# Row maxima turned in aligned groups and split off VectorE, sequence products kept for the last T blocks, and the output projection's operands loaded elsewhere

## The chip, the cores and the metric

The kernel runs on 1 core of one Trainium2 chip. The metric is the device time of one launch in microseconds; three runs of the kernel before gave 730.19, 731.53 and 732.51 us, a median of 731.53. The engines are named as in the profile: PE (matrix products; PEld its weight loads), DVE (VectorE), ACT (ScalarE), POOL (GpSimd) and SP (SyncE, which here only issues DMAs).

## The reference

Two mixers of one input x (2048 rows of 512) are added with a gate per row.

```python
def _A_ref(x, dft_seq_re, dft_seq_im, dft_hid_re, dft_hid_im):
    a = jnp.einsum("bsd,ed->bse", x, dft_hid_re)
    b = jnp.einsum("bsd,ed->bse", x, dft_hid_im)
    return jnp.einsum("ts,bse->bte", dft_seq_re, a) - jnp.einsum("ts,bse->bte", dft_seq_im, b)

def _B_ref(x, wqkv, wo):
    H = 32; Dh = D // H; W = 256
    ...
    scores = jnp.einsum("bhqd,bhkd->bhqk", q, k) * (Dh ** -0.5)
    mask = (idx[:, None] - idx[None, :] >= 0) & (idx[:, None] - idx[None, :] < W)
    p = _softmax(jnp.where(mask[None, None], scores, -1e9), axis=-1)
    o = jnp.einsum("bhqk,bhkd->bhqd", p, v)
    return (lambda x, *d: x.transpose(*d))(o, 0, 2, 1, 3).reshape(B, S, D) @ wo

g = _sigmoid((x * gate_w).sum(-1, keepdims=True))
return g * a + (1 - g) * b
```

A is a Fourier transform along the hidden and then the sequence dimension. B is attention with 32 heads of 16 in a window of 256 keys, and an output projection by wo.

## The kernel before

All large products take operands that are split into a high and a low part ("hl": a copy rounded to fp32r, and the rest), and add three of the four partial products (TERMS).

**Order.** One Python loop, `for n in range(N + LAG + 1)` (L938), writes the program out. N is 128: 8 sets of four heads by 16 blocks of 128 queries. Step n emits the four heads of **S block** n (`s_head`, L404: scores of one query block against its keys, and on DVE the row's extremum over the masked scores) and of **T block** n - 9 (`t_head`, L462: the scores again, transposed, with the row's extremum folded into the product by two more rows of the operand, and the exponential on ACT). LAG = 9 blocks lie between. From n = 128 there are T blocks alone. After four T blocks `pv` (L486) multiplies exponentials and values, once POOL has masked them (`t_mask`, L475).

Between the heads `fill` (L918) takes steps of a generator, `dense` (L672): first the q, k and v projections and the hidden transform, then ("proj" done) the sequence transform, 16 blocks of 24 steps (`c_block`, L646). One step is a pair of matmuls on the two halves of the rows (L246). The rate is a constant per stage (FILL_PROJ 1.55, FILL_SEQ 2.3 steps per half head). `defer(ticks, fn)` puts an instruction off by so many ticks, where each dense step is one tick and each half head 0.7: ticks set the place in the program, not a time. All engines work their own queue in order, and SP issues nearly all DMAs in order.

**Maxima.** `s_head` writes the four heads' extrema as columns of a 128x16 tile `nm`. Every four blocks `m_rows` (L424) negates them into a high part (L427, TENSOR_SCALAR) and a low part (L428, SCALAR_TENSOR_TENSOR), turns the 128x32 tile by a DVE transposition (L430), writes it to DRAM (m_scr) and 12 ticks later reads it back as rows 48 and 49 of `ring0`, where the T blocks' products take it. The groups begin at n = 9, 13, 17 and so on; one that crosses a sequence end is read in two parts.

**Projection.** The sum over the T blocks passes through DRAM: u_scr, packing into l_scr (row sums) and o_scr, reciprocals (L527), and back. For each quarter of the rows (sb 0 to 3) `o_load` (L841) loads four tiles of o and of the reciprocals, multiplies them on DVE 16 ticks later (L854) and splits them on ACT (L102) and DVE (L105); sb 1 and 2 start when the sequence products are done ("seq"), sb 3 when attention is. `wo_run` (L873) then makes output block tb: 12 matmuls, and one DVE instruction that adds the gated transform r (L893), which `wo_get` loads from r_scr into `fin` (in ring0's place) by SP.

Of the kernel before, what the change touches and what calls it, by code (L numbers as in the profile page):

```python
# [21 lines left out]
NS = 8  # L22
# [6 lines left out]
NPT = 7  # L29
FILL_FIRST, FILL_PROJ, FILL_SEQ = 4.0, 1.55, 2.3  # L30
TERMS = ((0, 0), (0, 1), (1, 0))
# [20 lines left out]
def fnet_window_mix(ctx: ExitStack, tc: tile.TileContext, xT, x, wqk, wv, wm, wx, cc, wo, gw, out):  # L52
# [14 lines left out]
    c_scr = [[dram.tile([P, U_W], F32, name=f"c_scr{c}_{q}") for q in range(4)] for c in range(4)]  # L67
    m_scr = [dram.tile([2, 2, 2, 4, 4, 32], F32, name=f"m_scr{i}") for i in range(NS * NB // 4 + 4)]
    l_scr = [[dram.tile([2, 16, 512], F32, name=f"l_scr{i}_{h}") for h in range(2)] for i in range(4)]
# [118 lines left out]
    for h in range(2):  # L188
        nc.gpsimd.memset(f(ring[1][64 * h + 32:64 * h + 64]), 1.0)

# [58 lines left out]
    def es_tile():  # L249
        return ev.tile([P, U_W], F32, name="es", bufs=3)  # L250

# [149 lines left out]

    ML = {}

    def s_head(n, j):  # L404
        p, h = divmod(j, 2)
        jb = n % NB
        u, jj = divmod(n - LAG, 4)
        if u not in ML:
            ML[u] = at.tile([P, 16], F32, name="nm")
            if not (0 <= LAG + 4 * u and LAG + 4 * u + 4 <= NS * NB):  # L410
                nc.vector.memset(ML[u], 0.0)
# [5 lines left out]
        nc.tensor.matmul(ps[:, :w], ring[0][r, p, jb * P:(jb + 1) * P], ring[1][r, p, k0:k0 + w],  # L417
                         start=True, stop=True)
        sm = at.tile([P, WIN], BF16, name="sm", bufs=1)
        nc.vector.tensor_tensor_reduce(out=sm[:, :w], in0=ps[:, :w], in1=mask[:, WIN - w:],  # L420
                                       scale=1.0, scalar=3e38, op0=OP.add, op1=OP.min,
                                       accum_out=ML[u][:, c:c + 1])

    def m_rows(u):  # L424
        m = ML.pop(u)
        hl = at.tile([P, 2, 16], F32R, name="mhl", bufs=1)
        nc.vector.tensor_scalar(hl[:, 0], m, -1.0, None, op0=OP.mult)  # L427
        nc.vector.scalar_tensor_tensor(hl[:, 1], m, -1.0, f(hl[:, 0]), op0=OP.mult, op1=OP.subtract)  # L428
        mt = at.tile([P, 32], F32, name="mt", bufs=1)
        nc.vector.transpose(mt, f(hl[:]).rearrange("q l c -> q (l c)"))  # L430
        ms = m_scr[u + LAG // 4 + 1]

        def write():
            ld(ms.rearrange("l h p b i q -> i (l h p b) q"), mt)
            defer(12, read)

        def read():
            b, end = max(0, LAG + 4 * u), min(NS * NB, LAG + 4 * u + 4)
            while b < end:
                e = min(end, (b // NB + 1) * NB)  # L440
                o = b - LAG - 4 * u
                for h in range(2):
                    ld(f(ring[0][64 * h + 48:64 * h + 50, :, b % NB * P:b % NB * P + (e - b) * P]),
                       ms[:, h, :, o:o + e - b].rearrange("l p b i q -> l p (b i q)"))
                b = e
        defer(2, write)

# [181 lines left out]

    order = CLEAR + [tb for p in PAIRED for tb in p]  # L630
    MRAW = {}
    MHL = {}
# [13 lines left out]
    def c_block(n, done):  # L646
        tb = order[n]
        clear = tb % 2 == 0
        pss = acc()
        hl = MHL.pop(n)  # L650
        m = 0
        for i in range(2):
            u = slice(0, H + 1) if i == 0 else slice(H, D + 1) if clear else slice(H + 1, 2 * H + 2)
            o = slice(H - 1, D) if clear and i else slice(0, H + 1)
            for q in range(4):
                k = (2 * q + i) * P
                for x, y in TERMS:
                    mm([ps[:, o] for ps in pss], hl[x][:, k:k + P], U[tb % 4, q][:, y, u], m == 0, m == 23,
                       True)
                    m += 1  # L660
# [180 lines left out]
    def o_load(sb, g):  # L841
        ls = l_scr[sb][g // 2]
        if sb == 3:
            t = pt_tile([P, 3, 512], F32R)
            o = f(t[:, 2])
        else:
            t = big_tile()[:, :, 0:512]
            o = f(t[:, 1])
        rl = RL[0][:, sb * 2 - 4 + g // 2, g % 2] if FIN and sb > 1 else es_tile()[:, 0:512]
        ld(rl, bass.AP(tensor=ls.tensor, offset=ls[1, g % 2 * 8].offset, ap=[[512, 8], [0, 16], [1, 512]]))  # L850
        ld(o, o_scr[sb][g])

        def product():
            nc.vector.tensor_mul(rl, o, rl)  # L854
            defer(4, high)

        def high():
            for c, p in TURNS:
                hi_of(by_class(t[:, 0])[:, c], rows_of(rl)[:, c, p])
            defer(4, low)  # L860

        def low():
            for c, p in TURNS:
                lo_of(by_class(t[:, 1])[:, c], rows_of(rl)[:, c, p], by_class(t[:, 0])[:, c])
            defer(8, OHL[sb].append, t)
        defer(16, product)

    def wo_get(tb):
        if tb in stored and tb not in wo_r:
            wo_r[tb] = FIN[0][:, tb % 8]  # L870
            ld(wo_r[tb], r_scr[tb])

    def wo_run():  # L873
# [11 lines left out]
        for q in range(0, 512, w):  # L885
# [7 lines left out]
            nc.vector.scalar_tensor_tensor(r[:, k], ps[:, :w], g0[:, tb:tb + 1], r[:, k], op0=OP.mult, op1=OP.add)  # L893
            defer(3 if tb == 15 else 8, ld, out[sb][:, c, k], r[:, k])
        wo_get(tb + 3)
# [211 lines left out]
```

## Time and profile before

| | us |
|---|---|
| median of 3 runs | 731.53 |
| profiled execution, its own time | 732.08 |
| its span in the trace | 730.2 |
| PE busy | 603.6 (83%) |
| DVE busy | 495.2 (68%) |
| POOL busy | 435.1 (60%) |
| ACT busy | 428.4 (59%) |

In the profile's rows "L427 DVE" is line 427 on VectorE; "out<-in" are the program's tile names; a bracket gives the idle time ahead of an instruction on its engine and what ended it. A matmul's end is modelled, so busy PE is not PE at its peak. In the windows, PEclk is the share of the TensorE clock that was granted. S blocks end at 619.8 us, the last T block's products at 662.0 us.

### The profile page before, as it was taken

How to read it: one execution, taken by the hardware profiler on the slowest of the kernel's cores; microseconds unless marked ns; L12 is line 12 of the kernel's file. 1: busy time of each engine (PE TensorE's matmuls, PEld its weight loads, DVE VectorE, ACT ScalarE, POOL GpSimd, SP SyncE). 2: the span in 40 equal slices, each digit the busy share in tenths (PEclk: the TensorE clock that was granted, in tenths of full speed). 3: DMA queues.
4: the chain of work that ended last, by engine and by line, in shares of the span. 5: the costliest groups of instructions: out<-in, count | busy, mean ns of one | idle time of the engine just before them, and what ended most of it. 6: DMA issues, size and time to landing. Idle time of an engine off the chain costs nothing. (4 is left out here: it accounts for less than half of the span.)

```text
span 730.2 us, 17617 instructions
## 1 busy us (share of the span) xinstructions
PE 603.6 (83%) x6222; PEld 450.6 (62%) x6222; DVE 495.2 (68%) x1419; ACT 428.4 (59%) x952; POOL 435.1 (60%) x521
## 2 busy tenths in 40 slices
PE   9999699899788898988868887769777799559885
PEld 6788466666454666665546566657666587437664
DVE  5278677787787788787766765675688677344561
ACT  6434578677556676665556767476667668652220
POOL 6012557676687766678584979988988746420000
PEclk9999889999999999889988897667779969858898
DMA  7777677787565778567586699856566743655883
GB/s 278 259 233 199 205 228 225 228 263 210 176 201 172 213 227 273 179 202 207 169 262 214 210 268 278 269 148 188 171 195 197 207 138 117 190 174 145 259 276 110
DMA packets 93605, 152.61 MB, mean 209 GB/s; under 512 B 33028, under 2 KB 42116, under 8 KB 93380
## 3 DMA queue, kind: packets, MB, share of 16 engines
q1 hardware_dynamic: 92068, 149.28, 66.9%
q10 hardware_dynamic: 1440, 2.10, 0.9%
q8 instruction: 53, 0.87, 0.6%
q14 instruction: 44, 0.36, 0.2%
HBM read 108.56 MB, written 47.24 MB: 213 GB/s over the span
## 5 line engine op out<-in xcount | busy, mean ns | idle before, releaser
L420 DVE CUSTOM_DVE_ANT_0 sm<-s,mask 128x384 bf16<-128x384 f32 (+2 forms) x512 | 270.3, 528 | 104.3 <-PE s L417 54.7
L473 ACT ACTIVATE pt<-t 128x384 f32<-128x384 f32 (+2 forms) x512 | 231.4, 474 | 101.1 <-PE t L472 77.8
L472 PE MATMUL t<-ring,ring 50*128 50x384 f32 (+2 forms) x512 | 218.3, 442 | 59.0 <-ACT pt L473 30.1
L246 PE MATMUL d<-big,hl 64*128 64x512 f32 (+2 forms) x1440 | 248.8, 384 | 0.5 <-DVE es L257 0.5
L417 PE MATMUL s<-ring,ring 48*128 48x384 f32 (+2 forms) x512 | 199.0, 400 | 33.0 <-DVE nm L420 28.7
L246 PEld LDWEIGHTS d<-big,hl 64*128 64x128 f32 x1440 | 177.0, 223 | 6.5 <-issue 1.7
L417 PEld LDWEIGHTS s<-ring,ring 48*128 48x128 f32 x512 | 106.2, 212 | 99.6 <-DVE nm L420 86.7
L479 POOL TENSOR_SCALAR_AFFINE_SELECT pt<-pt 128x512 f32<-128x512 f32 x128 | 83.0, 649 | 140.5 <-ACT pt L473 140.0
L472 PEld LDWEIGHTS t<-ring,ring 50*128 50x128 f32 x512 | 108.1, 214 | 91.3 <-ACT pt L473 46.4
L246 PE MATMUL d<-hl,big 64*128 64x512 f32 x600 | 111.7, 416 | 0.0
L498 PE MATMUL o<-pt,vpad 64*32 64x320 f32 (+5 forms) x2816 | 89.2, 392 | 15.9 <-POOL pt L479 10.8
L498 PEld LDWEIGHTS o<-pt,vpad 64*32 64x32 f32 x2816 | 69.1, 117 | 38.4 <-POOL pt L479 13.6
L339 POOL TENSOR_TENSOR cv<-cv 128x256 f32<-128x256 f32 (+1 forms) x64 | 74.4, 1163 | 20.4 <-DMA cv<-cc 16.9
L483 POOL TENSOR_SCALAR_AFFINE_SELECT pt<-pt 128x512 f32<-128x512 f32 x112 | 74.8, 667 | 0.0
L246 PEld LDWEIGHTS d<-hl,big 64*128 64x128 f32 x600 | 67.1, 195 | 4.8 <-issue 1.0
L504 ACT COPY es<-o 128x512 f32<-128x512 f32 x32 | 18.8, 586 | 82.0 <-PE o L498 77.9
L342 POOL TENSOR_TENSOR cv<-cv 128x512 f32<-128x512 f32 x48 | 62.9, 1311 | 0.0
L540 ACT ACTIVATE cv<-cv 128x768 f32<-128x768 f32 x72 | 60.6, 842 | 0.6 <-POOL cv L339 0.6
L505 DVE TENSOR_TENSOR es<-o,es 128x512 f32<-128x512 f32 x32 | 22.0, 688 | 43.2 <-ACT es L504 35.9
L105 POOL TENSOR_TENSOR hl<-es,hl 128x512 fp32r<-128x512 f32 x14 | 18.5, 1319 | 48.0 <-ACT hl L102 48.0
L105 POOL TENSOR_TENSOR hl<-raw,hl 128x512 fp32r<-128x512 f32 x35 | 45.4, 1309 | 2.2 <-ACT hl L102 2.2
L242 PE MATMUL t<-big 128*128 128x512 f32 x144 | 40.0, 438 | 8.1 <-DVE fin L893 8.1
(98 smaller groups left out, 648.3 us busy)
## 6 DMA issues: line engine op xcount, KB each, us to landing
cv<-cc SPq DMA_DIRECT2D x64, 512.0 KB
qk_scr<-hl SPq DMA_DIRECT2D x32, 512.0 KB
ring<-qk_scr SPq DMA_DIRECT2D x128, 128.0 KB
ring<-qk_scr SPq DMA_DIRECT2D x128, 64.0 KB
u_scr<-es SPq DMA_DIRECT2D x32, 256.0 KB
raw<-cc SPq DMA_DIRECT2D x16, 512.0 KB
fin<-r_scr SPq DMA_DIRECT2D x17, 256.0 KB
big<-c_scr SPq DMA_DIRECT2D x16, 258.0 KB
```

Of the source, the lines that this page charges most:

```text
L105: (nc.gpsimd if pool else nc.vector).tensor_sub(lo, raw, f(hi))
L246: nc.tensor.matmul(pss[h], w[r], x[r], start=start, stop=stop, skip_group_check=skip)
L339: (nc.gpsimd if pool else nc.vector).tensor_sub(out, a, b)
L342: (nc.gpsimd if pool else nc.vector).tensor_add(out, a, b)
L417: nc.tensor.matmul(ps[:, :w], ring[0][r, p, jb * P:(jb + 1) * P], ring[1][r, p, k0:k0 + w], start=True, stop=True)
L420: nc.vector.tensor_tensor_reduce(out=sm[:, :w], in0=ps[:, :w], in1=mask[:, WIN - w:], scale=1.0, scalar=3e38, op0=OP.add, op1=OP.min, accu ...
L472: nc.tensor.matmul(ps[:, :w], ring[1][r, p, q0:q0 + P], ring[0][r, p, q0:q0 + w], start=True, stop=True)
L473: nc.scalar.activation(pt[:, j, :w], ps[:, :w], AF.Exp, scale=-1.0)
L479: nc.gpsimd.affine_select(a, a, pattern=[[0, 4], [1, P]], compare_op=OP.is_ge, fill=0.0, base=0, channel_multiplier=-1)
L483: nc.gpsimd.affine_select(a, a, pattern=[[0, 4], [-1, P]], compare_op=OP.is_gt, fill=0.0, base=0, channel_multiplier=1)
L498: nc.tensor.matmul(ot[h][32 * j:32 * j + 32, a - sb * 512:e - sb * 512], v2[r, j], pt[r, j, a - kb * P:e - kb * P], start=kb == kbs[0], st ...
L540: nc.scalar.activation(junk, src, AF.Abs, accum_out=dst)
```

## The change

1. **Maxima.** The groups are aligned (n = 0, 4, 8 ...), and a group is turned at the start of the next block. DVE only transposes the raw 128x32 tile (one fixed tile NM, half of it zeros). ACT then copies the turned tile into the high part, POOL subtracts for the low part, and SP writes both, one DMA each; the reads are two per group. The constant rows of ring1 are -1 instead of 1, so nothing has to be negated.
2. **Sequence products.** In the S blocks the rate is set so that 48 steps are left at n = 128; these are spread over the last nine T blocks. After the last S block there are 49 steps in the program, where there were 36.
3. **Projection.** r for tb 0 to 2 is loaded from n = 132 on into the tiles T; for the other tb the load is issued by ACT. Of quarters 0 to 2 the reciprocals land in the high half of the operand tile and the product goes to an `es` tile, 24 ticks after the load. Stores of the output stand 13 ticks behind, not 8. A load of r_scr0 that was issued twice is issued once.

```diff
-FILL_FIRST, FILL_PROJ, FILL_SEQ = 4.0, 1.55, 2.3
+FILL_FIRST, FILL_PROJ, SEQ_END = 4.0, 1.55, 48
...
-        nc.gpsimd.memset(f(ring[1][64 * h + 32:64 * h + 64]), 1.0)
+        nc.gpsimd.memset(f(ring[1][64 * h + 32:64 * h + 64]), -1.0)
...
     def m_rows(u):
-        m = ML.pop(u)
-        hl = at.tile([P, 2, 16], F32R, name="mhl", bufs=1)
-        nc.vector.tensor_scalar(hl[:, 0], m, -1.0, None, op0=OP.mult)
-        nc.vector.scalar_tensor_tensor(hl[:, 1], m, -1.0, f(hl[:, 0]), op0=OP.mult, op1=OP.subtract)
         mt = at.tile([P, 32], F32, name="mt", bufs=1)
-        nc.vector.transpose(mt, f(hl[:]).rearrange("q l c -> q (l c)"))
+        nc.vector.transpose(mt, NM)
+        hl = at.tile([P, 2, 32], F32R, name="mhl", bufs=1)
+        defer(2, hi_of, hl[:, 0], mt)
+        defer(4, minus, hl[:, 1], mt, f(hl[:, 0]))
...
         def write():
-            ld(ms.rearrange("l h p b i q -> i (l h p b) q"), mt)
-            defer(12, read)
+            for l in range(2):
+                ld(ms[l].rearrange("z h p b i q -> i (z h p b) q"), f(hl[:, l]))
+            defer(9, read)
...
-        defer(2, write)
+        defer(7, write)
...
         for tb in range(3):
-            defer(1 + 6 * tb, wo_get, tb)
+            wo_get(tb)
...
-        rl = RL[0][:, sb * 2 - 4 + g // 2, g % 2] if FIN and sb > 1 else es_tile()[:, 0:512]
+        rl = RL[0][:, g // 2, g % 2] if sb == 3 else f(t[:, 0])
...
         def product():
-            nc.vector.tensor_mul(rl, o, rl)
-            defer(4, high)
+            to = rl if sb == 3 else es_tile()[:, 0:512]
+            nc.vector.tensor_mul(to, o, rl)
+            defer(4, high, to)
...
-        defer(16, product)
+        defer(16 if sb == 3 else 24, product)
...
-            wo_r[tb] = FIN[0][:, tb % 8]
-            ld(wo_r[tb], r_scr[tb])
+            wo_r[tb] = T[tb][:, 0:D] if tb < 3 else FIN[0][:, tb % 8]
+            (ld if tb < 3 else nc.scalar.dma_start)(wo_r[tb], r_scr[tb])
...
-            defer(3 if tb == 15 else 8, ld, out[sb][:, c, k], r[:, k])
+            defer(3 if tb == 15 else 13, ld, out[sb][:, c, k], r[:, k])
...
-        rate = FILL_FIRST if n < LAG else FILL_SEQ if "proj" in have else FILL_PROJ
+        if n < LAG:
+            rate = FILL_FIRST
+        elif "proj" not in have:
+            rate = FILL_PROJ
+        elif n < N:
+            rate = max(0, left[0] - SEQ_END) / (4 * (N - n) - 2)
+        else:
+            rate = left[0] / (4 * (N + LAG - n) - 2) if n < N + LAG else 0
...
+        if n >= N + 4:
+            for tb in range(3):
+                wo_get(tb)
...
+        if n % 4 == 0 and 0 < n <= N:
+            m_rows(n // 4 - 1)
...
-                defer(3, t_mask, k)
+                defer(3 if n < N else 1, t_mask, k)
...
-            if p == 0 and k % 4 == 0 and k // 4 - 1 in ML:
-                defer(3, m_rows, k // 4 - 1)
```

What this moves, as the built programs have it. First DVE at the end of a group of four blocks in the sequence stage (sm is the masked score, thrown away; nm the extrema), before:

```order
L420 ISA nm 128x1
L420 ISA sm,nm<-s,mask 128x256
L420 ISA nm 128x1
L427 TENSOR_SCALAR mhl<-nm 128x16
L428 SCALAR_TENSOR_TENSOR mhl<-nm,mhl 128x16
L430 STREAM_TRANSPOSE mt<-mhl 128x32
L420 ISA sm,nm<-s,mask 128x256
L420 ISA nm 128x1
```

and now, on DVE and then on POOL (pt are exponentials that are masked, cv blocks of the transform's matrices that are compared):

```order
L417 ISA sm,nm<-s,mask 128x384
L417 ISA nm 128x1
L423 STREAM_TRANSPOSE mt<-nm 128x32
L417 ISA sm,nm<-s,mask 128x384
L417 ISA nm 128x1
```

```order
L471 AFFINE_SELECT pt<-pt 128x4x128
L475 AFFINE_SELECT pt<-pt 128x4x128
L342 TENSOR_TENSOR cv<-cv 128x2x256
L339 TENSOR_TENSOR mhl<-mt,mhl 128x32
L339 TENSOR_TENSOR cv<-cv 128x2x128
L342 TENSOR_TENSOR cv<-cv 128x2x256
```

Two DVE instructions have gone, and the low part stands in POOL's queue among masks and comparisons. Second, ACT among the last T blocks (with buffer numbers; es_9787 and its like are products of the projection's operands, t the scores, o the attention's result), before:

```order
L473 ACTIVATE pt_9861<-t_9884 128x384
L102 CAST big_9786<-es_9787 128x384
L102 CAST big_9786<-es_9787 128x128
L473 ACTIVATE pt_9906<-t_9907 128x384
L473 ACTIVATE pt_9906<-t_9910 128x384
L102 CAST big_9845<-es_9846 128x384
L102 CAST big_9845<-es_9846 128x128
L473 ACTIVATE pt_9906<-t_9929 128x384
L473 ACTIVATE pt_9906<-t_9932 128x384
L749 ACTIVATE es_9939<-d0_9756 128x258
```

and now:

```order
L465 ACTIVATE pt_9869<-t_9893 128x384
L465 ACTIVATE pt_9869<-t_9896 128x384
L102 CAST big_9782<-es_9878 128x384
L102 CAST big_9782<-es_9878 128x128
L496 COPY es_9953<-o_9903 128x512
L465 ACTIVATE pt_9969<-t_9970 128x384
L465 ACTIVATE pt_9969<-t_9973 128x384
L102 CAST big_9812<-es_9958 128x384
L102 CAST big_9812<-es_9958 128x128
```

The first copies (CAST) of the projection's operands stand some three T blocks later; before, there are eight tiles of them ahead of the last T block's result, now four. Third, SP at the end of attention (u_scr3 is the last result's store), before:

```order
L96 DMA u_scr3_1_181<-es_10188 128x512
L96 DMA es_10193<-l_scr2_0_170 128x1x512
L96 DMA big_10192<-o_scr2_184 128x512
L96 DMA fin_10196<-r_scr0_186 128x512 x2
L96 DMA rl_10197<-l_scr2_1_171 128x1x512
L96 DMA big_10208<-o_scr2_184 128x512
L96 DMA fin_10196<-r_scr1_187 128x512
L96 DMA l_scr3_1_173<-u_scr3_1_181 16x512
```

and now:

```order
L96 DMA u_scr3_1_177<-es_10111 128x512
L96 DMA l_scr3_1_169<-u_scr3_1_177 16x512
L96 DMA o_scr3_181<-u_scr3_1_177 16x8192
L96 DMA l_scr2_1_167<-lt_10113 128x64
L96 DMA big_10148<-l_scr1_0_164 128x1x512
L96 DMA big_10148<-o_scr1_179 128x512
L96 DMA big_10151<-l_scr2_0_166 128x1x512
L96 DMA big_10151<-o_scr2_180 128x512
L96 DMA r_scr13_195<-ev_9884 128x512
```

The last quarter's packing has moved up, and the loads of quarters 1 (l_scr1, o_scr1) and 2, which stood among the T blocks, now come behind it. Fourth, DVE in the projection (es_10253 to es_10274 are products of quarters 1 and 2, rl those of quarter 3), now:

```order
L849 TENSOR_TENSOR es_10272<-big_10213 128x512
L849 TENSOR_TENSOR es_10274<-big_10216 128x512
L105 TENSOR_TENSOR pt_10225<-rl_10118,pt_10225 128x384
L105 TENSOR_TENSOR pt_10225<-rl_10118,pt_10225 128x128
L849 TENSOR_TENSOR rl_10118<-pt_10242,rl_10118 128x512
L105 TENSOR_TENSOR big_10213<-es_10272,big_10213 128x384
L105 TENSOR_TENSOR big_10213<-es_10272,big_10213 128x128
```

The product of quarter 3's second tile (pt_10242) stands ahead of the low part of quarter 1's last tile (big_10213); before, quarter 1 was through on DVE before the last T block's result.

More of the change, by code (lines that the diff above doesn't have):

```diff
@@ L67, in fnet_window_mix @@
     c_scr = [[dram.tile([P, U_W], F32, name=f"c_scr{c}_{q}") for q in range(4)] for c in range(4)]
-    m_scr = [dram.tile([2, 2, 2, 4, 4, 32], F32, name=f"m_scr{i}") for i in range(NS * NB // 4 + 4)]
+    m_scr = [dram.tile([2, 2, 2, 2, 4, 4, 32], F32, name=f"m_scr{i}") for i in range(NS * NB // 4)]
     l_scr = [[dram.tile([2, 16, 512], F32, name=f"l_scr{i}_{h}") for h in range(2)] for i in range(4)]
@@ L249, in es_tile @@
     def es_tile():
-        return ev.tile([P, U_W], F32, name="es", bufs=3)
+        return ev.tile([P, D], F32, name="es", bufs=3)
     def collect(pss, then, scale=1.0):
@@ L400, in u_split @@
         defer(4, lo_of, t[:, 1], f(t[:, 1]), t[:, 0], True)
-    ML = {}
+    NM = const.tile([P, 32], F32, name="nm")
+    nc.gpsimd.memset(NM, 0.0)
     def s_head(n, j):
@@ L406, in s_head @@
         jb = n % NB
[L407 to L411, printed above, removed]
+        u, jj = divmod(n, 4)
         c = (h * 2 + p) * 4 + jj
@@ L421, in s_head @@
                                        scale=1.0, scalar=3e38, op0=OP.add, op1=OP.min,
[L422 removed]
+                                       accum_out=NM[:, c:c + 1])
     def m_rows(u):
[L425 to L428 removed]
         mt = at.tile([P, 32], F32, name="mt", bufs=1)
[L430 to L431 removed]
+        nc.vector.transpose(mt, NM)
+        hl = at.tile([P, 2, 32], F32R, name="mhl", bufs=1)
+        defer(2, hi_of, hl[:, 0], mt)
+        defer(4, minus, hl[:, 1], mt, f(hl[:, 0]))
+        ms = m_scr[u]
         def write():
[L434 to L435 removed]
+            for l in range(2):
+                ld(ms[l].rearrange("z h p b i q -> i (z h p b) q"), f(hl[:, l]))
+            defer(9, read)
         def read():
[L438 to L445, printed above, removed]
[L446 removed]
+            b = u % 4 * 512
+            for h in range(2):
+                ld(f(ring[0][64 * h + 48:64 * h + 50, :, b:b + 512]), ms[:, 0, h].rearrange("l p b i q -> l p (b i q)"))
+        defer(7, write)
     PT = {}
@@ L630, in fnet_window_mix @@
     order = CLEAR + [tb for p in PAIRED for tb in p]
+    left = [16 * 24]
     MRAW = {}
@@ L659, in c_block @@
                        True)
+                    left[0] -= 1
                     m += 1
```

10 lines of the change are left out of this document (5 added, 5 removed).

## The prediction

> **What bounds the kernel now.** I read the windows first, then the PE's waits stage by stage, then the timelines at the longest waits. In the windows each engine has its busy time and count; PEclk is the granted clock.
>
> ```profile
> core 0: us, PE busy (x) PEld busy (x) DVE busy (x) ACT busy (x) POOL busy (x), PEclk, DMA share, GB/s
> 456.00:476.00 20.00, 13.74 (x175) 11.97 (x175) 14.29 (x24) 10.64 (x24) 20.00 (x24) 0.67 0.83 250
> 596.00:616.00 20.00, 18.60 (x260) 14.23 (x241) 13.62 (x47) 13.67 (x31) 9.43 (x14) 0.95 0.42 130
> 619.80:640.00 20.20, 11.45 (x190) 9.31 (x187) 8.66 (x18) 13.95 (x34) 8.39 (x13) 0.80 0.62 185
> 640.00:662.00 22.00, 14.86 (x207) 10.87 (x207) 9.64 (x16) 11.21 (x28) 5.16 (x8) 0.50 0.51 161
> 662.00:706.00 44.00, 35.89 (x134) 27.11 (x134) 22.98 (x39) 11.45 (x19) 0.00 (x0) 0.91 0.73 231
> 706.00:730.20 24.20, 15.48 (x72) 12.77 (x70) 5.55 (x9) 0.00 (x0) 0.00 (x0) 0.80 0.46 156
> ```
>
> There are three stages. Up to 619.8 us S blocks (with their maxima) and T blocks (exponentials) run together, and the PE is the fullest engine wherever nothing stalls (18.60 of 20 us). From 619.8 to 662.0 only T blocks are left and the PE is half idle. From 662.0 the output projection runs, up to 730.2. These are the PE's waits in the first stage (total us, times, longest):
>
> ```profile
> PE s L417 <- DVE nm L420: 28.7, 39, 5.0
> PE t L472 <- DMA ring<-m_scr: 17.9, 12, 5.8
> PE t L472 <- ACT pt L473: 16.0, 25, 2.0
> PE o L498 <- POOL pt L479: 10.8, 6, 3.7
> ```
>
> The largest is for DVE. What holds DVE is the turning of the maxima; per line: shortest, median and longest ns.
>
> ```profile
> L427 DVE TENSOR_SCALAR mhl<-nm x33: 162/532/11735, 41.3 to 624.9; 128x16 fp32r<-128x16 f32 x33
> L428 DVE SCALAR_TENSOR_TENSOR mhl<-nm,mhl x33: 174/549/1269, 41.5 to 625.2; 128x16 fp32r<-128x16 f32 x33
> L430 DVE STREAM_TRANSPOSE mt<-mhl x33: 211/211/214, 41.7 to 625.4; 128x32 f32<-128x32 f32 x33
> ```
>
> The same 16 columns take 0.16 us or 11.73 us, while the transposition never varies. The longest, on DVE and then on POOL:
>
> ```profile
> 467.07 11.73 DVE L427 TENSOR_SCALAR mhl<-nm 128x16 fp32r<-128x16 f32 x1
> ```
>
> ```profile
> 477.50 1.27 POOL L339 TENSOR_TENSOR cv<-cv 128x512 f32<-128x512 f32 x1
> ```
>
> POOL, busy 20.00 of the 20 us to 476, ends a run of work at 478.77; L427 ends at 478.80. So L427 waits until POOL has a pause, not for one instruction. On the PE the three longest cost:
>
> ```profile
> 479.63 0.58 PE L417 MATMUL s<-ring,ring 48*128 48x256 f32 x1 [4.99 <-DVE nm L420]
> ...
> 542.43 0.44 PE L417 MATMUL s<-ring,ring 48*128 48x384 f32 x1 [2.20 <-DVE nm L420]
> ...
> 560.04 0.40 PE L417 MATMUL s<-ring,ring 48*128 48x256 f32 x1 [2.87 <-DVE nm L420]
> ```
>
> **Part 1: the maxima.** L427 and L428 go; DVE keeps the transposition, whose 211 ns are the same beside a busy POOL, so I expect no wait in their place. The three rows above come to 10.1 us of PE idle; the rest of those DVE stalls lay under other products. Off that path are 30 more pairs with a median of 0.53 and 0.55 us. What they cost the PE is not shown singly: between nothing and the other 28.7 - 10.1 = 18.6 us of waits for DVE. I take 5, near the lower end, since most of those waits come from the maxima themselves (L420). **Part 1: -15.1 us** (bounds -10 and -29).
>
> Added per group of four blocks: a copy on ACT and a subtraction on POOL, both 128x32, and a second write on SP. The nearest row, of eight times the size (busy us, mean ns):
>
> ```profile
> L460 POOL COPY vpad<-vr 128x256 f32<-128x256 f32 x32 | 13.4, 418 | 0.0
> ```
>
> At most 0.4 us each, 32 times: 13 us on each of two engines that idle for 6 and 11 of the 20 us from 596, so I count nothing, unless POOL is behind. But the chain to the ring rows now passes POOL's queue, and SP stands at the write until POOL has subtracted, with all loads behind it. Against that the groups are turned at a block's start rather than some way into it: the first use comes three blocks later (33 turnings from 41.3 to 624.9 us are 18.2 us per group, 4.6 per block, so 13.7 us). The waits of 17.9 us for these rows I leave as they are; bounds -10 and +15.
>
> At this place the Trainium skill's page "SBUF — State Buffer", section "Who interferes with whom", says that VectorE and GpSimd share a port pair, held for one whole instruction, the second comer blocking until it ends. By that, L427 could wait for at most one POOL instruction, here 1.27 us; the trace shows 11.73 us, so the measurement decides.
>
> **Part 2: the stage of T blocks alone.** The PE there:
>
> ```profile
> 622.68 2.49 PE L498 MATMUL o<-pt,vpad 64*32 64x64 f32 x96
> ...
> 627.20 0.92 PE L246 MATMUL d<-big,hl 64*128 64x258 f32 x9
> ...
> 636.57 2.37 PE L472 MATMUL t<-ring,ring 50*128 50x384 f32 x6 [7.25 <-ACT pt L473]
> 640.52 1.06 PE L472 MATMUL t<-ring,ring 50*128 50x384 f32 x2 [1.58 <-ACT pt L473]
> 642.81 4.89 PE L498 MATMUL o<-pt,vpad 64*32 64x64 f32 x96 [1.23 <-ACT pt L473]
> 647.63 3.17 PE L472 MATMUL t<-ring,ring 50*128 50x384 f32 x8
> 651.60 0.75 PE L472 MATMUL t<-ring,ring 50*128 50x128 f32 x2 [0.80 <-ACT pt L473]
> 656.80 0.74 PE L472 MATMUL t<-ring,ring 50*128 50x128 f32 x2 [4.45 <-ACT pt L473]
> 657.47 4.52 PE L498 MATMUL o<-pt,vpad 64*32 64x64 f32 x96
> 661.92 11.74 PE L242 MATMUL t<-big 128*128 128x512 f32 x48
> ```
>
> The waits named come to 7.25 + 1.58 + 1.23 + 0.80 + 4.45 = 15.3 us. The same 96 products take 2.49 us while sequence products fill the gaps and 4.89 and 4.52 us after they ran out, at a clock of 0.50. ACT is late because copies for the projection stand in its queue ahead of exponentials, and wait for operands that have not landed:
>
> ```profile
> 630.33 1.19 ACT L102 CAST big<-es 128x384 fp32r<-128x384 f32 x2 [2.16 <-DVE es L854]
> ```
>
> After the change only the first quarter's operands are loaded and split in this stage: the second and third need "seq" done, and the sequence products (49 pairs after the last S block instead of 36) now last to the stage's end. The first quarter's product is placed 24 ticks after its load instead of 16. So the 15.3 us go, except some 2 us for operands that still land late; the products run warm (-4.4 us); 13 more pairs cost 2.6 us (9 matmuls took 0.92 us). 42.2 - 15.3 + 2 - 4.4 + 2.6 = 27.1 us. **Part 2: -15.1 us** (bounds -11 and -18).
>
> **Part 3: the projection gives much of it back.** Before, the second quarter's operands were in place when the last T block ended, and the PE ran almost without a pause from 661.92 to 721.5 us. Now the second and third quarters' loads are issued only behind the last attention result's write, interleaved tile by tile, and the fourth's directly behind. Counting from the last attention product's end: copy and add 1.3, write to DRAM and two packing transfers, so first loads at about 6 us. DVE is in order: the product of the fourth quarter's second tile stands ahead of the last low part of the second quarter. So the second quarter is ready only when 20 loads of 256 KB, four prefetches of r and some writes have moved, about 7.6 MB. The GB/s from 600 us to the end, in forty slices, and one load's landing in the chain of waits:
>
> ```profile
> GB/s 243 205 0 10 114 181 172 18 225 204 329 178 184 163 5 159 293 227 64 71 260 168 157 331 260 320 88 226 352 288 332 236 137 348 325 130 113 88 15 8
> ```
>
> ```profile
> 692.03 7.26 DMA pt<-o_scr
> ```
>
> At 231 GB/s (the window from 662) 7.6 MB take 33 us, at 352, the fullest slice, 22 us; I take 26, since the loads stand in one unbroken queue.
>
> With 1.3 us for product and low part the second quarter is ready at 6 + 26 + 1.3 = 33 us. The first quarter needs 11.7 us, so the PE stands still for some 21 us. Then twelve blocks:
>
> ```profile
> 705.66 4.32 PE L242 MATMUL t<-big 128*128 128x512 f32 x12 [1.82 <-DVE fin L893]
> 709.78 11.70 PE L242 MATMUL t<-big,pt 128*128 128x512 f32 x60
> ```
>
> A block takes 2.93 us (11.74 / 4) and the first after a pause 4.32: 12 x 2.93 + 1.4 = 36.6. The last product to the span's end is 8.7 us as now (721.5 to 730.2). 33 + 36.6 + 8.7 = 78.3 us against 68.2. **Part 3: +10.1 us** (bounds +5 with 28 us, +17 with 40). The r tiles read early into T, the double load of r_scr0 that goes, and the loads on ACT's queue cost nothing: they lie under this gap.
>
> **Sum.** 730.2 - 15.1 - 15.1 + 10.1 = 710.1 us of span. The profiled execution took 732.08, 1.9 more than its span, and the runs' median 731.53 is 0.55 below that: 711.5 us.
>
> **Rivals.**
> *The projection eats the gain.* With loads at 200 GB/s the second quarter is ready at 45 us, and part 3 is +22: span 722, time 723.5. For it: 161 to 185 GB/s in the windows before 662. Against: 231 and 252 where loads queue up. Chance 0.17.
> *The wait isn't freed.* Either POOL itself, full from 456 to 476, becomes the bound and its masks (10.8 us of PE waits) take the place of the maxima, or L427's wait is not POOL's doing and the transposition, now first in its place, inherits it. Part 1 is then worth 0, the span 725, the time 726.5. For: POOL at 20.00 of 20. Against: L427's end 0.03 us after POOL's, and the transposition's 214 ns at most. Chance 0.12. (The rule of the Trainium skill quoted above is on this rival's side: a wait of 11.73 us would not be that of the port.)
> *Slower: the ring rows come late.* POOL's subtraction waits behind its backlog (up to the 11.73 us that DVE waited), then come two transfers. If that passes 13.7 us in most groups, each T block that opens a group waits; at the present mean of 17.9 / 12 = 1.5 us in all 32 groups it is 48 us instead of 17.9: span 740, time 742. It decides once POOL is some 7 us behind, with 3 us per transfer. For: POOL at 20.00 of 20. Against: it idles half the time at 596. Chance 0.11.
> The forecast has 0.60.
>
> **Range.** Part 1 at -24, part 2 at -17 and part 3 at +5.5 give a span of 694.7 and a time of 696; all the best ends together would give less, but rarely meet. Upward the range covers the first two rivals, to 729, and leaves out the slower one. About 0.3% is what a measurement here can tell from no change: 2.2 us. Faster 0.84, same 0.05 (the ends of the first two rivals), slower 0.11.
>
> **What would show it.** Right: no DVE instruction at the groups' ends over 0.25 us; PE waits for DVE under 20 us in the first stage; T blocks alone in about 27 us; one PE gap of about 20 us after four blocks of the projection. Wrong: waits for the rows of maxima well over 18 us, SP standing at their write, masks that hold the PE for over 20 us, or a gap over 30 us in the projection.

## The result and the profile after

The changed kernel takes 742.18 us (median of 4 runs, 739.41 to 743.37) beside 731.72 us before: a ratio of 1.014 (95% interval 1.0106 to 1.0174). It is 1.4% slower, where 711.5 us, and with a chance of 0.84 a gain, were forecast. Ratios here and below compare fast runs only, since some executions of the same program take 1.5% longer or more. The profiled execution has a span of 741.7 us, 11.5 more than before. Its windows by stage (last S product 620.9, last attention product 657.0, second quarter ready at 701):

```profile
core 0: us, PE busy (x) PEld busy (x) DVE busy (x) ACT busy (x) POOL busy (x), PEclk, DMA share, GB/s
0.00:620.90 620.90, 526.31 (x5596) 382.46 (x5596) 396.41 (x1271) 391.07 (x900) 427.28 (x531) 0.90 0.70 212
620.90:657.30 36.40, 27.42 (x424) 21.81 (x422) 10.98 (x23) 22.41 (x57) 14.49 (x23) 0.77 0.50 149
657.30:701.00 43.70, 18.64 (x62) 12.07 (x61) 19.61 (x35) 13.11 (x24) 0.00 (x0) 0.68 0.72 226
701.00:741.70 40.70, 32.24 (x145) 26.43 (x145) 14.52 (x23) 2.67 (x5) 0.00 (x0) 0.92 0.42 139
```

Against before, the first stage is 1.1 us longer (619.8), the T blocks alone take 36.4 us (42.2), and from there to the end 84.4 us pass (68.2): +1.1 - 5.8 + 16.2 = 11.5 us. The forecast for the three was -15.1, -15.1 and +10.1. These are single executions: the first stage of one and the same program took 619.8 us in the kernel before and 623.6 in p3_proj below. The PE's waits of the first stage, which were 28.7, 17.9, 16.0 and 10.8 us before:

```profile
PE s L414 <- DVE nm L417: 24.3, 37, 2.9
PE t L464 <- ACT pt L465: 18.5, 22, 4.6
PE t L464 <- DMA ring<-m_scr: 17.6, 5, 6.7
PE o L490 <- POOL pt L471: 9.7, 8, 5.3
...
PE t L464 <- DVE nm L417: 5.5, 10, 1.8
```

The long stalls of DVE are gone, as is what made them; the turn that is left takes its 0.21 us each time:

```profile
L423 DVE STREAM_TRANSPOSE mt<-nm x32: 198/211/214, 53.8 to 621.9; 128x32 f32<-128x32 f32 x32
```

But PE stands as long as before: 94.6 us of the stage (93.8 before). Its waits for DVE fall only from 28.7 to 24.3 us, although the three long ones, 10.1 us, are gone: the others grew from 18.6 to 24.3. And the rows now hang on POOL's queue. The third group, in order of time (in brackets the wait):

```profile
83.48 0.21 DVE L423 STREAM_TRANSPOSE mt<-nm 128x32 f32<-128x32 f32 x1
83.83 0.21 ACT L102 CAST mhl<-mt 128x32 fp32r<-128x32 f32 x1
84.43 7.67 SPq L96 DMA_DIRECT2D m_scr<-mhl  x2
...
88.34 1.83 POOL L339 TENSOR_TENSOR cv<-cv 128x768 f32<-128x768 f32 x1 [6.62 <-DMA cv<-cc]
...
91.31 0.25 POOL L339 TENSOR_TENSOR mhl<-mt,mhl 128x32 fp32r<-128x32 f32 x1
92.20 4.98 SPq L96 DMA_DIRECT2D ring<-qk_scr  x8
98.65 0.64 SPq L96 DMA_DIRECT2D ring<-m_scr  x2
103.92 0.65 PE L464 MATMUL t<-ring,ring 50*128 50x384 f32 x1 [6.74 <-DMA ring<-m_scr]
```

POOL subtracts 7.5 us after ACT's copy, SP stands at the two writes for 7.67 us, then come eight ring loads that the alignment has put between write and read, and the rows are 6.7 us late. POOL was not overloaded here: it stood 6.62 us at a comparison whose load had not landed, and the subtraction stands behind that in its queue. In six more of the 32 groups the subtraction comes over 3 us after the copy, with POOL busy all the while. One of them is at the second of the three long stalls (6.90 us of DVE at 534.57 before), now:

```profile
528.95 8.24 SPq L96 DMA_DIRECT2D m_scr<-mhl  x2
534.06 1.06 ACT L532 ACTIVATE cv<-cv 128x1024 f32<-128x1024 f32 x1 [2.95 <-POOL cv L339]
536.39 0.26 POOL L339 TENSOR_TENSOR mhl<-mt,mhl 128x32 fp32r<-128x32 f32 x1
537.25 0.68 PE L464 MATMUL t<-ring,ring 50*128 50x384 f32 x1 [4.58 <-ACT pt L465]
```

ACT waits for POOL's comparison with exponentials queued behind it, so at this place PE waits for ACT instead of for DVE.

### The profile page after: what moved, and what is told of

Read it like the earlier page. It is cut to its first block, busy times and chain, and to the rows that moved or that the text cites. A ratio compares the mean times of both kernels' runs of the same rounds, so it can differ in the third digit from the quotient of the medians.

```text
span 741.7 us, 17664 instructions
## 1 busy us (share of the span) xinstructions
PE 604.6 (82%) x6222; PEld 442.8 (60%) x6222; DVE 441.5 (60%) x1350; ACT 429.3 (58%) x984; POOL 441.8 (60%) x554
## 4 chain that ended last, share of the span: by engine, by line
PE 39%; DMA 17%; DVE 14%; POOL 12%; issue 7%; ACT 7%; SPq 3%; DVEq 0%; POOLq 0%; ACTq 0%
PE d L246 12%; DVE sm L417 8%; PE o L490 7%; PE s L414 5%; PE t L242 5%; PE d L242 4%; PE t L464 4%; SPq L96 3%; DMA ring<-qk_scr 3%; DMA cv<-cc 2%; POOL cv L342 2%; DMA big<-l_scr 2%; DMA raw<-cc 2%; ACT pt L465 2%; POOL hl L105 2%
## 5 line engine op out<-in xcount | busy, mean ns | idle before, releaser
L464 PE MATMUL t<-ring,ring 50*128 50x384 f32 (+2 forms) x512 | 215.5, 432 | 56.6 <-ACT pt L465 25.4
L414 PE MATMUL s<-ring,ring 48*128 48x384 f32 (+2 forms) x512 | 199.5, 400 | 30.3 <-DVE nm L417 24.3
L246 PEld LDWEIGHTS d<-big,hl 64*128 64x128 f32 x1440 | 175.0, 216 | 7.2 <-issue 2.4
L414 PEld LDWEIGHTS s<-ring,ring 48*128 48x128 f32 x512 | 103.3, 205 | 103.5 <-DVE nm L417 88.7
L464 PEld LDWEIGHTS t<-ring,ring 50*128 50x128 f32 x512 | 104.8, 207 | 88.8 <-ACT pt L465 38.8
L246 PE MATMUL d<-hl,big 64*128 64x512 f32 x600 | 108.4, 406 | 0.0
L490 PE MATMUL o<-pt,vpad 64*32 64x320 f32 (+5 forms) x2816 | 92.7, 397 | 14.6 <-POOL pt L471 9.7
L342 POOL TENSOR_TENSOR cv<-cv 128x512 f32<-128x512 f32 x48 | 62.8, 1308 | 10.2 <-DMA cv<-cc 10.2
L246 PEld LDWEIGHTS d<-hl,big 64*128 64x128 f32 x600 | 65.1, 190 | 3.4 <-issue 1.0
L242 PEld LDWEIGHTS t<-big 128*128 128x128 f32 x144 | 28.8, 205 | 35.7 <-DVE big L105 15.4
```

What stands on the lines that cost most here:

```text
L242: nc.tensor.matmul(pss[0], w, x, start=start, stop=stop, skip_group_check=skip)
L246: nc.tensor.matmul(pss[h], w[r], x[r], start=start, stop=stop, skip_group_check=skip)
L342: (nc.gpsimd if pool else nc.vector).tensor_add(out, a, b)
L464: nc.tensor.matmul(ps[:, :w], ring[1][r, p, q0:q0 + P], ring[0][r, p, q0:q0 + w], start=True, stop=True)
L490: nc.tensor.matmul(ot[h][32 * j:32 * j + 32, a - sb * 512:e - sb * 512], v2[r, j], pt[r, j, a - kb * P:e - kb * P], start=kb == kbs[0], st ...
```

## The experiments

Each was timed against the kernel before on the same chip. The sequence part alone was not tried: as I read the program, beside the old projection its loads would wait for `es` tiles that only later instructions free.

### The parts one by one

p1_maxima is before with change 1 alone, p3_proj with change 3 alone, a_old_rate the changed kernel with the old rate (changes 1 and 3):

```diff
-            rate = max(0, left[0] - SEQ_END) / (4 * (N - n) - 2)
...
+        rate = FILL_FIRST if n < LAG else FILL_SEQ if "proj" in have else FILL_PROJ
```

> The kernel before with the maxima's part of the change alone. Theory 1 (the low part waits in POOL's queue, SP stands at its write, and eight ring loads stand between write and read, so that the late rows eat what the stalls of DVE gave): no gain, 730 to 735 us, with the last S block's product as late as in the changed kernel (620.9 us) and over 15 us of PE waits for rows of m_scr. Rival (the prediction's part 1 is right, and what ate it is in the other parts): 715 to 721 us, last S product near 605 us.

Measured: 1.0141 (1.0105 to 1.0176). The maxima by themselves cost some 10 us, more than either side had. The last S product comes at 624.0 us.

> The kernel before with the projection's part alone: the sequence products still end early, so quarters 1 and 2 are still loaded among the T blocks. Theory (the projection is late only because 'seq' comes late): 728 to 734 us, no gap over 5 us on PE in the projection. Rival (the loads of r on ACT's queue, or the product 8 ticks later, cost by themselves): 736 to 742 us, with ACT standing at a load of r.

Measured: 0.9889 (0.9846 to 0.9933), a gain of 8 us that no part of the forecast had: T blocks alone 38.6 us, last attention product to last product 56.3 us (59.5 before).

> The changed kernel without its sequence part (rate 2.3 as before). Theory (the late 'seq' costs 16 us in the projection and gains 6 among the T blocks): 730 to 734 us, some 10 us below the changed kernel, T blocks alone in about 42 us, projection in 68 to 70. Rival (the sequence part is worth its gain and the projection is late for its own loads): 740 us or more.

Measured: 0.9967 (0.9925 to 1.001). Without the new rate the T blocks alone take 35.5 us, as with it, and the projection 54.8 us instead of 76.2. So the gain among the T blocks belongs to the projection's part, and the sequence part only costs: 1.7% between these two kernels (1.014 and 0.9967), more than the whole loss.

### Why the projection is late

s_early ends the sequence products four T blocks sooner; s_recip_late puts the last group's reciprocal 30 ticks later in DVE's queue:

```diff
-            rate = left[0] / (4 * (N + LAG - n) - 2) if n < N + LAG else 0
+            rate = left[0] / (4 * (N + LAG - 4 - n) - 2) if n < N + LAG - 4 else 2.3
...
-            defer(d, l_inv, lt)
+            defer(d + 30 if FIN else d, l_inv, lt)
```

> The changed kernel with the sequence products spread over the first five of the last nine T blocks instead of all nine, so that 'seq' is done four blocks earlier. Theory (quarters 1 and 2 are late only because their loads wait for 'seq'): projection 55 to 62 us instead of 76, T blocks alone 36 to 40, time 728 to 733, ratio 0.995 to 1.002. Rival (the last group's reciprocal, or the loads' rate, sets it): projection 70 us or more, ratio 1.010 or more.

Measured: 0.9944 (0.99 to 0.9987). Projection 56.2 us, its first seven blocks in one piece:

```profile
665.19 19.76 PE L242 MATMUL t<-big 128*128 128x512 f32 x84
688.89 4.34 PE L242 MATMUL t<-big 128*128 128x512 f32 x12 [3.94 <-DVE fin L888]
```

The T blocks alone take 41.7 us, so the four last ones run without filling; what matters is that the loads of quarters 1 and 2 lie among them.

> The changed kernel with the reciprocal of the last group's sums put 30 ticks later in DVE's queue. If DVE's stand of 9.4 us at it holds up quarters 1 and 2: the second quarter is ready 6 to 9 us earlier, projection 67 to 71 us instead of 76, ratio 1.003 to 1.008. If the loads' rate sets it: projection 74 us or more, ratio 1.012 to 1.016.

Measured: 1.006 (1.0024 to 1.0095), projection 69.2 us. In the changed kernel DVE stood at the reciprocal, whose load stands behind several of quarters 1 and 2 on SP, with the low parts queued behind it:

```profile
682.29 0.55 DVE L519 RECIPROCAL lt<-lt 128x64 f32<-128x64 f32 x1 [9.39 <-DMA lt<-l_scr]
...
683.33 2.14 DVE L105 TENSOR_TENSOR big<-es,big 128x384 fp32r<-128x384 f32 x4
...
694.30 0.69 DVE L849 TENSOR_TENSOR rl<-pt,rl 128x512 f32<-128x512 f32 x1 [3.83 <-DMA pt<-o_scr]
```

In s_recip_late the first of these low parts still starts only at 683.04 us, 23.6 us after the last attention product instead of 26.2. Most of the gain comes later, where the last quarter's products (the third row) no longer stand on DVE between those of quarter 1. So some 7 of the 21 us (76.2 less 54.8) are DVE's order, and s_early, with its loads among the T blocks, takes 20 away.

### What the maxima cost: the rows

m_low_dve takes the low part back to DVE; m_read_first also brings the read ahead of the ring loads; m_read_pool does so with the low part on POOL (2 ticks instead of 3). The edit of m_read_first, against p1_maxima; m_low_dve has of it only the `False`, which puts the subtraction on DVE:

```diff
-        defer(2, hi_of, hl[:, 0], mt)
-        defer(4, minus, hl[:, 1], mt, f(hl[:, 0]))
+        defer(1, hi_of, hl[:, 0], mt)
+        defer(3, minus, hl[:, 1], mt, f(hl[:, 0]), False)
...
-            defer(9, read)
+            defer(3, read)
...
-        defer(7, write)
+        defer(4, write)
```

> The maxima's part alone (as p1_maxima, which took 1.014 of the kernel before) with the low part subtracted by DVE instead of POOL. Theory A (POOL's queue makes the rows late): ratio 1.000 to 1.006, no group in which SP stands over 3 us at the second write, waits for m_scr under 10 us. Rival B (the eight ring loads between write and read do): 1.012 to 1.016, waits for m_scr still 15 us or more.

Measured: 1.0209 (1.0154 to 1.0264). The waits for rows fall from 15.2 us to 4.5, so POOL's queue did make them late; but DVE stalls again (its subtraction took up to 14.7 us), and PE waits for that instead (22.6 us in p1_maxima):

```profile
PE s L414 <- DVE nm L417: 39.9, 47, 12.7
...
PE t L464 <- DMA ring<-m_scr: 4.5, 3, 2.6
```

> As m_low_dve, and high part, low part, write and read brought to 1, 3, 4 and 7 ticks after the turn, so that in all 32 groups the read stands ahead of the eight ring loads. Theory B: waits for m_scr under 3 us, time 6 us or more below m_low_dve, ratio 0.985 to 0.998. Theory A: no further gain over m_low_dve. Rival C (what the maxima lose is not the rows but the time of PE's products itself, through the granted clock): waits for m_scr gone, and the ratio still above 1.005.

Measured: 1.0161 (1.0075 to 1.0247), within m_low_dve's interval: bringing the read forward gives nothing that can be told, though the waits for rows are down to 1.5 us. That is the sign of rival C; how much the clock has to do with it is taken up in the last section.

> The maxima's part alone (1.014) with the low part on POOL as in the change, but high part, low part, write and read at 1, 2, 4 and 7 ticks, so that the read stands ahead of the eight ring loads. If those loads delay the rows: waits for m_scr under 8 us (15.2 in p1_maxima), ratio 1.003 to 1.010. If POOL's queue alone does: 12 us or more, ratio 1.012 or more, and the ring loads stand behind SP's wait for POOL.

Measured: 1.0163 (1.0099 to 1.0226). PE waits for rows 1.6 us instead of 15.2 in p1_maxima, and T products for ACT 34.5 us instead of 18.0. Late rows are thus not what the maxima lose: take them away, and the next wait comes up.

p1_ring_later emits the ring loads a block later, behind the reads:

```diff
-        ring_ahead(n + 1)
+        if n < LAG:
+            ring_ahead(n + 1)
...
+        if n >= LAG:
+            ring_ahead(n + 1)
```

> The maxima's part alone, with the eight ring loads of a group emitted at the end of a block's step instead of its start, so that the reads of the maxima's rows stand ahead of them on SP. Theory 1: the rows land some 6 us earlier, the waits for m_scr fall from about 17 us to under 6, and the time is 6 to 12 us below p1_maxima. Rival (POOL's queue alone sets when the rows come, or S products now wait for their ring): within 3 us of p1_maxima or slower.

Measured: 1.0311 (1.0264 to 1.0358). No product waits for rows any more, but S products now wait 38.3 us for their ring, as the rival had it. So its time says nothing on what the rows are worth.

### What the maxima cost: the place of the turn

m_split_dve has the change's groups with the old split on DVE; g_unsplit the old groups with the change's unsplit turn and split by ACT and POOL; b_turn_first is before with the turn put at the start of the step. Their edits, against p1_maxima, before and before:

```diff
-        nc.vector.transpose(mt, NM)
...
+        nc.vector.tensor_scalar(hl[:, 0], m, 1.0, None, op0=OP.mult)
+        nc.vector.scalar_tensor_tensor(hl[:, 1], m, 1.0, f(hl[:, 0]), op0=OP.mult, op1=OP.subtract)
+        nc.vector.transpose(mt, f(hl[:]).rearrange("q l c -> q (l c)"))
```

```diff
-            ML[u] = at.tile([P, 16], F32, name="nm")
+            ML[u] = NM[:, u % 2 * 16:u % 2 * 16 + 16]
...
-        nc.vector.tensor_scalar(hl[:, 0], m, -1.0, None, op0=OP.mult)
-        nc.vector.scalar_tensor_tensor(hl[:, 1], m, -1.0, f(hl[:, 0]), op0=OP.mult, op1=OP.subtract)
...
+        nc.vector.transpose(mt, NM)
+        defer(2, hi_of, hl[:, 0], mt)
+        defer(4, minus, hl[:, 1], mt, f(hl[:, 0]))
```

```diff
-            if p == 0 and k % 4 == 0 and k // 4 - 1 in ML:
-                defer(3, m_rows, k // 4 - 1)
...
+        if k % 4 == 0 and k // 4 - 1 in ML:
+            m_rows(k // 4 - 1)
```

> Aligned groups as in the change, but the maxima split on DVE ahead of the turn and written by one DMA, as before (write 2, read 14 ticks behind). If the alignment costs (ring loads now between write and read): ratio 1.008 or more and the L427-like stalls of up to 11 us still there. If the split off DVE costs (ACT, POOL, two writes): ratio 0.997 to 1.003.

Measured: 1.0232 (1.0161 to 1.0304). Aligned groups cost 2.3% with the old instructions; the unsplit turn wins some of it back (1.0141 in p1_maxima, though the intervals overlap).

> The kernel before with its own groups (a group is turned beside a pv, behind the ring loads on SP), but turned unsplit and split by ACT and POOL, with two writes, as in the change. Theory D (the alignment is what costs: the turn no longer lies beside pv's products, and the ring loads come between write and read): ratio 0.982 to 0.996, waits for DVE in the S products under 22 us, none over 3 us. Rival A (POOL's late low part costs whatever the groups): 1.004 or more, waits for m_scr above 18 us.

Measured: 1.0017 (0.9982 to 1.0053). Both signs of the theory came, its time did not:

```profile
PE s L417 <- DVE nm L420: 20.7, 35, 1.6
```

L427 and L428 are gone, no wait for DVE is longer than 1.6 us, and yet in the old groups the unsplit turn is worth nothing that can be told. It doesn't cost either, so against p1_maxima the aligned groups cost 1.2%.

> The kernel before, with nothing changed but that the turn of the maxima stands at the start of the block's step, three heads earlier than before and so away from the attention products (old groups, split on DVE). Theory F (those products covered DVE's 1.3 us per group, and without them PE waits): waits of S products for DVE over 40 us instead of 28.7, ratio 1.006 or more. Rival (the rows' chain and SP's order are what the alignment costs): the rows come earlier, waits for m_scr fall under 12 us, ratio 1.002 or less.

Measured: 1.035 (1.0296 to 1.0404): 25 us for a step that stands three heads earlier, with no instruction added. In the kernel before, the turn of a group (DVE) and the attention products (PE):

```profile
110.97 0.62 DVE L427 TENSOR_SCALAR mhl<-nm 128x16 fp32r<-128x16 f32 x1
111.62 1.21 DVE L428 SCALAR_TENSOR_TENSOR mhl<-nm,mhl 128x16 fp32r<-128x16 f32 x1
112.87 0.21 DVE L430 STREAM_TRANSPOSE mt<-mhl 128x32 f32<-128x32 f32 x1
```

```profile
110.58 2.46 PE L498 MATMUL o<-pt,vpad 64*32 64x64 f32 x96
```

DVE's 2.1 us lie under 2.46 us of products that did not wait for DVE. In b_turn_first, DVE and PE:

```profile
105.84 0.60 DVE L427 TENSOR_SCALAR mhl<-nm 128x16 fp32r<-128x16 f32 x1
106.47 1.02 DVE L428 SCALAR_TENSOR_TENSOR mhl<-nm,mhl 128x16 fp32r<-128x16 f32 x1
107.53 0.21 DVE L430 STREAM_TRANSPOSE mt<-mhl 128x32 f32<-128x32 f32 x1
```

```profile
108.11 0.68 PE L472 MATMUL t<-ring,ring 50*128 50x384 f32 x1 [2.17 <-DVE nm L420]
109.15 4.26 PE L498 MATMUL o<-pt,vpad 64*32 64x64 f32 x96
```

The same work is now bare, and the attention products come behind it, at half the clock (0.50 from 106.2 to 113.0 us). Over the first stage (to 647.8 us):

```profile
PE s L417 <- DVE nm L420: 55.3, 50, 10.8
...
PE t L472 <- DVE nm L420: 10.3, 11, 2.2
```

28.7 and 3.1 us have become 55.3 and 10.3, though no product waits for rows any more (17.9 before). The longest wait goes from 5.0 to 10.8 us: L427's longest stall (11.96 us here) is bare as well.

### POOL's backlog

The r kernels take both low parts of the sequence operands (hl<-raw, 32 of 1.3 us) from POOL to DVE: r_before in the kernel before, r_p1 in p1_maxima, r_split in m_split_dve, r_p3 in p3_proj, r_g in g_unsplit_proj (g_unsplit with change 3).

```diff
-            MHL[n] = split_raw(MRAW.pop(n), at_, step, 2)
+            MHL[n] = split_raw(MRAW.pop(n), at_, step, 0)
```

> The kernel before with the same move from POOL to DVE. Theory E: L427 no longer waits 11.7, 6.9 and 4.9 us, since POOL has pauses; ratio 0.985 to 0.996. Rival (DVE is the tighter engine, and the low parts stall there beside POOL as L427 does): 1.004 or more.

Measured: 0.984 (0.978 to 0.99), some 12 us for one changed argument; the medians of all runs, 725.85 and 734.80 us, give 9.

> The maxima's part alone (p1_maxima, 1.014), with both low parts of each sequence operand (hl<-raw, 32 of 1.3 us among the last 40 blocks) on DVE instead of POOL. Theory E (POOL's backlog holds PE whatever stands behind it): the low part of the maxima is no longer late after 400 us, waits of PE for masks, ACT and m_scr after 400 us fall from some 35 us to under 20, ratio 0.990 to 1.003. Rival (the alignment and the granted clock): 1.010 or more.

Measured: 1.0078 (1.0044 to 1.0113), 0.6% better than p1_maxima, less than the theory had.

> Aligned groups with the split on DVE (m_split_dve, 1.023) and POOL relieved of the 41 us (the kernel before so relieved: 0.984). If the alignment costs by itself, without backlog and without late rows: 1.000 or more. If what it cost was the longer stalls of DVE at POOL's backlog: 0.980 to 0.992.

Measured: 1.0197 (1.0149 to 1.0246). Against r_before's 0.984, the alignment costs 3.6% even without the backlog, with the split on DVE.

> The projection's part alone (0.989) with the same move. Theory E: 0.975 to 0.986. Rival: 0.992 or more.

Measured: 0.9773 (0.9706 to 0.9839), 719.12 us. It beats both kernels: the change's projection part and one split moved from POOL, with neither the maxima nor the sequence part. L427 takes 1.29 us at most, not 11.73:

```profile
L427 DVE TENSOR_SCALAR mhl<-nm x33: 156/512/1286, 40.2 to 614.2; 128x16 fp32r<-128x16 f32 x33
```

> The same with the projection's part of the change added (0.989 by itself). Theory D: the two gains add up, ratio 0.972 to 0.986. Rival A: 0.990 or more.

Measured: 0.995 (0.9902 to 0.9999), on the rival's side: the unsplit turn adds nothing to the projection's part.

> The unsplit turn in the old groups and the projection's part (0.995), with the same move. Theory E: 0.972 to 0.985, the best version of all. Rival: 0.993 or more.

Measured: 0.9884 (0.9822 to 0.9947). Not the best version: with POOL relieved, the unsplit turn in the old groups comes out 1.1% behind DVE's split (r_p3), though the intervals touch.

## Why the prediction was wrong

**Part 1, -15.1 us, measured +1.1 in the profile and about +10 alone.** Two steps failed. The first is the worth of the stalls itself, "10.1 us of PE idle" and 5 more, with "I count nothing" for the work added on ACT and POOL. In g_unsplit, where only the split has moved, PE's waits for DVE fall by 8.0 us and the time doesn't change. The second is "Against that the groups are turned at a block's start rather than some way into it": I counted the new place as slack for the rows, and did not look at what PE did beside the old one. With the old instructions the place alone is worth 25 us (b_turn_first): there the attention products no longer cover DVE's 2.1 us.

The change, though, leaves DVE only 0.21 us per group, so b_turn_first doesn't price it. For the change itself the runs show 1.2% between p1_maxima and g_unsplit, and its path stays open. Single profiles don't settle it. In the first stage of p1_maxima PE idles 88.0 us and is busy 536.0; in that of a_old_rate, whose program is the same up to there, 95.1 and 531.7; in that of g_unsplit 87.0 and 530.1. Nor is it in the waits for rows (15.2, 17.1 and 14.5 us).

That L427 waits for pauses of POOL is shown by its 1.29 us in r_p3. But the 1.6% of r_before is not L427's alone: from p3_proj to r_p3, PE's waits for DVE fall from 30.5 to 20.7 us, and those for masks and ACT together from 25.6 to 17.1. The change leaves POOL's queue as it is. The second rival (0.12) had part 1 worth nothing, but by masks or by the transposition, and neither came: masks hold PE for 9.7 us (10.8 before), the turn takes 0.21 us. I also priced each wait at its length alone, which the last section takes up.

**Part 2, -15.1 us, measured -5.8, and none of it by the sequence products.** That the exponentials would no longer stand behind the projection's copies was half right (2.11 and 4.12 us of waits for ACT were left). The step that failed is "except some 2 us for operands that still land late": the late one is the reciprocal of the row sums ahead of the product, on DVE, and ACT's copies stand behind that product.

```profile
648.47 0.55 DVE L519 RECIPROCAL lt<-lt 128x64 f32<-128x64 f32 x1 [4.72 <-DMA lt<-l_scr]
648.94 0.63 DVE L849 TENSOR_TENSOR es<-big 128x512 f32<-128x512 f32 x1
```

```profile
649.60 1.20 ACT L102 CAST big<-es 128x384 fp32r<-128x384 f32 x2 [3.86 <-DVE es L849]
```

"The products run warm" (at the full clock) failed as well: PE is busy 27.42 of 36.4 us, its clock 0.77, and the three sets of 96 products took 4.89, 2.69 and 3.81 us.

**Part 3, +10.1 us, measured +16.2.** The mechanism was right, down to which quarter is late. The step that failed is the term "26" for the loads: the second quarter was ready 43.7 us after the last attention product, not 33. The loads ran at 226 GB/s in that stretch, where 26 us for 7.6 MB ask for 292, and the reciprocal's load, behind several of them, held DVE for 9.39 us. "The loads on ACT's queue cost nothing" was not safe either. The late sequence products write the last r late, and ACT stood at its load:

```profile
662.37 11.37 ACTq L866 DMA_DIRECT2D fin<-r_scr  x2
```

In a_old_rate and s_early these issues take under 1 us. With the reciprocal out of the way (s_recip_late), DVE stands for an r loaded by that queue:

```profile
682.37 0.75 DVE L888 SCALAR_TENSOR_TENSOR fin<-t,g,fin 128x512 f32<-128x512 f32 x1 [7.67 <-DMA fin<-r_scr]
```

What these stands cost by themselves no run shows. The upper bound (+17) held the +16.2. The first rival (45 us) comes near the moment, but its rate of 200 GB/s was not what was measured.

**The rivals.** The slower one gave 742 us, which is what was measured, but not by its mechanism: waits for the ring rows stayed at 17.6 us, in 5 places and not 32. The number was right by chance. Of the signs of being right, only the short turn came: PE's waits for DVE are 24.3 us and not under 20, the T blocks take 36.4 us and not 27, and PE's pause in the projection is in pieces of up to 8.24 us. Of the signs of being wrong, SP stands at the write of the maxima (7.67 and 8.24 us).

## What to carry to other kernels

Before moving an engine's work in a tight loop, look up what the bound engine does beside it at the old place and at the new one: whether it is covered depends on the place, not on the work. Here a stall behind a full engine was cured at that engine (one split moved off POOL brought 1.6%), not by moving the victim's work onto engines that queue behind the same one (nothing, in g_unsplit). And the work whose end starts loads (here "seq") should not be spread over the stage that is meant to hide those loads.

## What the runs showed of the hardware

A wait of PE can cost more than its length. In the kernel before, one product waited 1.10 us, and the clock in windows of 3.4 us around it was:

```profile
105.47 0.41 PE L472 MATMUL t<-ring,ring 50*128 50x384 f32 x1 [1.10 <-DMA ring<-m_scr]
```

```profile
103.00:106.40 3.40, 2.12 (x16) 1.54 (x17) 2.05 (x8) 2.46 (x8) 2.16 (x3) 0.99 0.86 282
106.40:109.80 3.40, 3.40 (x22) 3.38 (x20) 2.81 (x11) 3.38 (x9) 1.49 (x2) 0.51 0.47 170
109.80:113.20 3.40, 3.40 (x107) 2.75 (x106) 2.82 (x7) 1.24 (x4) 3.40 (x5) 1.00 0.75 193
```

PE idled 1.28 of 3.4 us, and the next 3.4 us ran at half the clock, up to 1.7 us lost on top. Windows of 0.2 us show 20 such stretches (before up to 450 us, after up to 260 us): 15 last 3.4 us, four 6.8 and one 10.2, and the PE idle in the 3.4 us ahead of each is 0.7 to 3.4 us. The other way round, in the first stage of the kernel before, cut at the clock's own steps: of the windows at the full clock with under 0.75 us of idle, none of 104 was followed by the half clock; of those with 1.75 us or more, all 9 were; in between, 14 of 28. The Trainium skill's page "TensorE: Matmul & The Clock Gate", section "What's actually happening", has the clock halved by default and released by activity, in windows of about 3.4 us; the length agrees with these rows. Its idle window of 3.4 us before the clock falls does not: here little over 1 us of idle within one was enough. So waits can be priced too low by their length. How far this goes, the first stage of b_turn_first and of the kernel before shows:

```profile
0.00:647.80 647.80, 544.57 (x5626) 390.66 (x5627) 445.56 (x1340) 390.55 (x874) 422.08 (x501) 0.88 0.67 203
```

```profile
0.00:619.80 619.80, 525.97 (x5626) 390.58 (x5627) 448.41 (x1340) 391.77 (x874) 421.50 (x501) 0.89 0.70 212
```

The same 5626 products keep PE busy 18.6 us longer, and it idles 9.4 us longer (103.2 and 93.8). The two add up to the 28 us of the stage. The stretches at half the clock come to 153.6 us, against 133.1 before: 20.5 us more, which explain at most 10.2 of the 18.6 us. What makes up the rest is not shown. Some of that spread is there without any change: in p3_proj, whose program is the same up to there, PE is busy 529.39 us to 623.6.
